# The last three attention slots of a two-part kernel reordered, and its routing cut by batch

## Chip, cores and metric

The kernel runs on one core of one Trainium2 chip. The metric is the device time of one execution in microseconds (us), the median of several runs. A core has a matrix engine (PE, with its weight loads shown as PEld), a vector engine (DVE), a scalar engine (ACT), GpSimd (POOL), SyncE (SP, which here only issues transfers) and 16 DMA engines that move data. Each engine works through its own list of instructions in order and waits on semaphores for the others. Matmul results land in PSUM, everything else lives in SBUF. "p_h<-xTt,w_all" in a profile row means that an instruction writes tile p_h and reads tiles xTt and w_all.

## What is computed

A chunked attention over 4 batches, 8 heads and 768 tokens is followed by a mixture of 8 experts with a noisy top-2 router over all 3072 tokens.

```python
for c in range(nc):                      # 24 chunks of 32 tokens; keys from 16 left to 8 right
    k_full = concat([mem_k, k[:, :, l_start:r_end]], axis=2)      # 8 memory keys + window
    scores = scale * matmul(q_c, k_full.T)
    a = softmax(scores)
    out[:, :, c_start:c_end] = matmul(a, v_full)
x = out.transpose(0, 2, 1, 3).reshape(N, D)                       # N = 3072, D = 512
noisy = x @ w_gate + log1p(exp(x @ w_noise)) * noise
top2 = the two largest of 8 per token; top2_w = softmax over the two
for e in range(E):                       # 8 experts
    h = maximum(x[mask] @ w1[e], 0.0)    # w1[e]: 512 x 1024
    out[mask] += top2_w[mask, k, None] * (h @ w2[e])              # w2[e]: 1024 x 512
```

## The kernel before, in words

Attention goes in 12 slots of 256 tokens, three to a batch: slots 0 to 2 are batch 0, and slots 9 to 11 batch 3. The rows of 128 tokens are called groups, two to a slot, 24 in all. For each slot `scores` runs 40 small matmuls into a PSUM tile ps_s, and DVE takes the row maximum (mx, L423) and subtracts it (sc, L425). `exps` is one ACT instruction (pb, L430). `turn_p` transposes the result on PE (L436), and ACT copies it to pT (L439). `values` sums the weights on PE (small, L447), multiplies with the values (ps_o, L453), and DVE normalises into xrow (L457, L460). `turn_x` transposes that on PE (L470), with a copy by ACT (xT, L472), and `gate` multiplies with the gate and noise weights (L480), whereupon DVE copies the logits to lg_all (L482). Before a batch can start, `turn` transposes its keys and queries ("turns", L393): 8 units, four of K and four of Q, each copied out by ACT or DVE (L549). There is one kT for all batches, so a batch's K copies wait until the scores of the batch before are done.

The engines PE, ACT, DVE and SP keep the order in which the program writes their instructions (a manual schedule), and POOL is pinned likewise. The loop over i = 0 to 11 at L562 is a pipeline: pass i makes the scores of slot i + 1, the turn_p of slot i, the turn_x of slot i - 1, the values of slot i, the exps of slot i + 1 and the gate of slot i - 1. `PLAN` puts the turns of the next batch into the passes; batch 3's K turns stand at the end of pass 7. ps_s and ps_o have one PSUM tile each, and all other PSUM tiles of the attention come from a ring of three (`bank`).

Routing is made in four `Route`s over groups: r0 (0 to 5), ra (6 to 13), rb (14 to 19) and rc (20 to 23). `choose` is 14 small DVE instructions that find the two experts and write a one-hot of the pair (ohp). `ranks` is a chain of small matmuls, `place` turns them into a rank per token, `total` carries the counts on, and `slots` writes a one-hot of the rank (oh_l). `weights` and `values` of a Route run on POOL or DVE. `lists` multiplies oh_l with the values into p_list on PE, and DVE adds that to `listed`. From `listed`, `decode` makes main_src, the token numbers to gather. `keep_x` writes xrow to DRAM (xd) as the source of the gathers.

POOL issues most transfers on one software queue: the loads of q, k and v, and then the weights of expert 0 before pass 6, of expert 1 before pass 7 and of expert 2 at the top of pass 8 (`load_expert`: w1 at L78, w2 at L79). Expert 2 lies in SBUF over the buffers of batch 3's K and Q, so its load waits for their turns on PE. Behind these loads POOL issues the first gathers (L671). The second part then runs step by step over pairs of experts: transposes p_xt (L691), matmuls p_h (L714) and p_y (L726).

Of the kernel before, what the change touches and what calls it, by code (L numbers as in the profile page):

```python
# [11 lines left out]
F32 = mybir.dt.float32  # L12
# [10 lines left out]
def kernel(  # L23
# [14 lines left out]
    nc = tc.nc  # L38
# [100 lines left out]
    ring = [0]  # L139
# [93 lines left out]
    class Route:  # L233
# [7 lines left out]
        def tile(self, name, width, dtype=F32):  # L241
            full = route.tile([128, self.home * width], dtype, name=f"{name}{self.home}")
            return full[:, 0:self.n * width]
# [158 lines left out]
    def scores(t):  # L402
        b, tp = divmod(t, TP)
        ps_s = psS.tile([128, 2, HP, 2, KW], F32, name="ps_s")
# [28 lines left out]
    def turn_p(pb):  # L433
# [4 lines left out]
        pT = work.tile([128, 2 * HP, 128], BF16, name="pT")  # L438
# [3 lines left out]
    def values(t, pT, between=None):  # L442
# [6 lines left out]
        ps_o = psO.tile([128, 2, HP, 2, D], F32, name="ps_o")  # L449
# [9 lines left out]
        for j in range(2):  # L459
            nc.vector.tensor_tensor(out=xr[:, j, 0:Dm].rearrange("p (h d) -> p h d", h=H),  # L460
                                    in0=ps_o[:, j].rearrange("p c a d -> p (c a) d"), in1=bc(rs[:, j], D), op=Alu.mult)
            if j == 0 and between is not None:
                between()
# [52 lines left out]
    with tc.manual_schedule(engines={ET.PE, ET.Activation, ET.DVE, ET.SP}):  # L516
# [34 lines left out]
        def fill(i, at):  # L551
            b, tp = divmod(i, TP)
            if b + 1 < B:
                turns(b + 1, PLAN[min(b, 1)].get((tp, at), ()))
# [4 lines left out]
                {(1, 1): QS[0:2], (1, 2): QS[2:4] + KS})  # L559

        r0, ra, rb, rc = Route(0, 6, 8), Route(6, 8, 8), Route(14, 6, 8), Route(20, 4, 4)
        for i in range(NT):  # L562
            b, tp = divmod(i, TP)
            last = i == NT - 1
            more = b + 1 < B

            if tp == 0 and more:
# [9 lines left out]
            if i == 2 * TP + 2:  # L577
                load_expert(2)
                ra.weights(nc.gpsimd)
                ra.order()  # L580
                ra.values(nc.gpsimd, 0, NV)
# [4 lines left out]
            if not last:  # L586
                sc = scores(i + 1)

            pTs[i] = turn_p(pbs.pop(i))
            if last:  # L590
                keep_x(b, 0, SO - 2, nc.scalar)
            elif i and tp == 0:
# [4 lines left out]
            xrs[i] = values(i, pTs.pop(i), (lambda: gate(i - 1, xTs_.pop(i - 1))) if last else None)  # L597
            if last:
                break
            pbs[i + 1] = exps(sc)  # L600
            if i in (TP + 2, 2 * TP + 2):
# [384 lines left out]
```

## Time and profile before

| what | us |
|---|---|
| median of the three runs (lowest, highest) | 358.08 (357.22, 363.62) |
| the profiled execution, its own time | 358.42 |
| its span, from the first to the last instruction | 356.7 |
| PE busy, share of the span | 285.9, 80% |
| DVE busy | 170.3, 48% |
| ACT busy | 136.9, 38% |
| POOL busy | 134.3, 38% |
| q0, the software queue that POOL issues: megabytes, share of the 16 DMA engines' time | 46.82 MB, 73.2% |
| PE p_h (L714) on the chain that ended last | 18% |
| PE p_y (L726) on that chain | 13% |

The profile is of one execution, and the durations in the text are its. The span is 1.7 us shorter than the execution's own time. A window's "DMA share" is the work of the 16 DMA engines over their time; packets can overlap, so that it can go over 1. PEclk is the share of the matrix engine's full clock that was granted.

### The profile page before, as it was taken

The numbers are of one execution on the slowest core, as the hardware profiler recorded it, in microseconds if no ns is written. First come the engines' busy times: TensorE is split into PE (matmuls) and PEld (weight loads), VectorE is DVE, ScalarE is ACT, GpSimd is POOL, SyncE is SP. The second block draws the span as 40 slices with busy tenths as digits, with TensorE's granted clock in tenths as the row PEclk, the third lists the DMA queues.
The fourth block names the chain that finished last, engine by engine and source line by source line (L and its number), as shares of the span: only waits on it lengthen the run. The fifth ranks groups of instructions, "written<-read, shape, count | busy, mean of one in ns | idle before, by whom it ended". The sixth has DMA issues, their size and how long they took to land.

```text
span 356.7 us, 7042 instructions
## 1 busy us (share of the span) xinstructions
PE 285.9 (80%) x2934; PEld 186.3 (52%) x2955; DVE 170.3 (48%) x349; ACT 136.9 (38%) x189; POOL 134.3 (38%) x181
## 2 busy tenths in 40 slices
PE   0356577777847732999999999999999999999991
PEld 0245455666736621865544465664455775565540
DVE  7656456699689885531133302954310334223221
ACT  8813645564645610144322343213243222243310
POOL 6460573354453036706530744332580122201122
PEclk9995655565687865699999999999999999999998
DMA  8999999999999999499999999961289971100012
GB/s 122 235 171 169 245 174 208 251 198 211 247 156 208 253 249 180 106 194 143 178 196 235 209 173 252 159 119 51 87 166 189 208 184 54 53 2 2 25 47 81
DMA packets 49866, 56.97 MB, mean 160 GB/s; under 512 B 16931, under 2 KB 39523, under 8 KB 49828
## 3 DMA queue, kind: packets, MB, share of 16 engines
q0 software_dynamic: 34240, 46.82, 73.2%
q1 hardware_dynamic: 13920, 6.62, 10.9%
q10 hardware_dynamic: 1668, 3.02, 2.4%
q8 instruction: 25, 0.41, 0.5%
q14 instruction: 13, 0.11, 0.1%
HBM read 70.39 MB, written 13.96 MB: 236 GB/s over the span
## 4 chain that ended last, share of the span: by engine, by line
PE 33%; issue 20%; POOL 5%; DVE 4%; DMA 3%; POOLq 1%; ACT 0%; DVEq 0%
PE p_h L714 18%; PE p_y L726 13%; POOL out_dram L677 4%; DMA out_dram<-y,main_dst 1%; DMA xTt<-xt 1%; DMA xt<-xd,main_src 1%; POOL xt L671 1%; DVE w_all L460 1%; PE p_xt L691 0%; POOL w_all L844 0%; POOLq L981 0%; DVE mx L423 0%; DVE sc L425 0%; ACT xT L472 0%; PE ps_o L453 0%
## 5 line engine op out<-in xcount | busy, mean ns | idle before, releaser
L714 PE MATMUL p_h<-xTt,w_all 128*128 128x256 bf16 (+3 forms) x669 | 102.7, 313 | 0.7 <-DVE xTt L692 0.5
L726 PE MATMUL p_y<-w_all,h 128*128 128x512 bf16 x446 | 102.3, 379 | 0.9
L714 PEld LDWEIGHTS <-w_all 128*128 128x128 bf16 x736 | 70.0, 101 | 36.3 <-issue 0.7
L702 ACT ACTIVATE h<-p_h 128x512 bf16<-128x512 f32 (+1 forms) x81 | 44.7, 551 | 95.9 <-PE p_h L714 88.3
L726 PEld LDWEIGHTS <-h 128*128 128x128 bf16 x464 | 45.3, 98 | 51.6
L700 DVE TENSOR_SCALAR h<-p_h 128x512 bf16<-128x512 f32 (+1 forms) x49 | 31.0, 633 | 82.8 <-PE p_h L714 73.7
L677 POOL DMA_INDIRECT out_dram<-y,main_dst x28 | 30.9, 1103 | 87.9 <-DVE y L732 75.4
L732 DVE SCALAR_TENSOR_TENSOR y<-p_y,main_w,y 128x512 f32<-128x512 f32 x28 | 21.0, 750 | 39.2 <-PE p_y L726 32.5
L393 PE MATMUL p_t<-identb,w_all 128*64 128x128 bf16 x384 | 20.6, 288 | 23.0 <-DMA w_all<-in_k_dram 13.4
L671 POOL DMA_INDIRECT xt<-xd,main_src x28 | 27.9, 997 | 24.2 <-DMA xTt<-xt 13.0
L730 ACT ACTIVATE y<-p_y,main_w 128x512 f32<-128x512 f32 x28 | 19.2, 687 | 37.0 <-PE p_y L726 36.0
L393 PEld LDWEIGHTS <-w_all 128*64 128x64 bf16 x384 | 18.1, 155 | 25.2 <-DMA w_all<-in_k_dram 13.9
L439 ACT COPY pT<-p_p 128x1024 bf16<-128x1024 bf16 x12 | 12.1, 1012 | 27.5 <-PE p_p L436 27.5
L383 POOL DMA_DIRECT2D w_all<-vd x16 | 11.8, 747 | 23.8 <-DMA vd<-vp 19.3
L460 DVE TENSOR_TENSOR w_all<-ps_o,rs 128x512 bf16<-128x512 f32 x24 | 15.6, 686 | 8.2 <-PE ps_o L453 7.8
L415 PE MATMUL ps_s<-kT,qT 128*32 128x112 bf16 x384 | 11.6, 276 | 7.2 <-DVE kT L549 5.4
L368 POOL COPY vp<-w_all 128x1536 bf16<-128x1536 bf16 x8 | 11.5, 1469 | 13.2 <-DMA w_all<-in_v_dram 13.2
L430 ACT ACTIVATE pb<-sc 128x1024 bf16<-128x1024 f32 x12 | 12.8, 1063 | 8.9 <-DVE sc L425 8.7
L549 DVE COPY kT<-p_t 64x768 bf16<-64x768 bf16 x12 | 11.5, 955 | 7.9 <-PE p_t L393 7.8
L425 DVE TENSOR_TENSOR sc<-ps_s,mx 128x1024 f32<-128x1024 f32 x12 | 14.7, 1225 | 0.8
L423 DVE TENSOR_REDUCE mx<-ps_s 128x16 f32<-128x1024 f32 x12 | 14.7, 1224 | 0.8 <-PE ps_s L415 0.5
L453 PE MATMUL ps_o<-w_all,pT 128*32 128x128 bf16 x384 | 10.9, 280 | 3.3 <-issue 2.0
(172 smaller groups left out, 284.0 us busy)
## 6 DMA issues: line engine op xcount, KB each, us to landing
w_all<-in_moe_w_dram POOLq DMA_DIRECT2D x16, 1024.0 KB, 20.7
w_all<-in_moe_w_dram POOLq DMA_DIRECT2D x8, 512.0 KB, 13.8
w_all<-in_v_dram POOLq DMA_DIRECT2D x4, 768.0 KB, 12.1
w_all<-in_k_dram POOLq DMA_DIRECT2D x4, 768.0 KB, 20.9
w_all<-in_q_dram POOLq DMA_DIRECT2D x4, 768.0 KB, 18.1
vd<-vp SPq DMA_DIRECT2D x4, 768.0 KB, 9.0
w_all<-vd POOLq DMA_DIRECT2D x8, 384.0 KB, 13.0
w_all<-vd POOLq DMA_DIRECT2D x8, 288.0 KB, 13.3
```

The lines of the kernel that those rows point to most:

```text
L393: nc.tensor.transpose(out=p_t[own(par), s, :], in_=src[:, 2 * pair + par, s * D:(s + 1) * D], identity=identb, tile_position=(0, par * 64))
L423: nc.vector.tensor_reduce(out=mx, in_=s3, axis=AX, op=Alu.max)
L425: nc.vector.tensor_tensor(out=sc, in0=s3, in1=bc(mx, KW), op=Alu.subtract)
L460: nc.vector.tensor_tensor(out=xr[:, j, 0:Dm].rearrange("p (h d) -> p h d", h=H), in0=ps_o[:, j].rearrange("p c a d -> p (c a) d"), in1=bc( ...
L671: i = nc.gpsimd.indirect_dma_start(out=xts[key].bitcast(I32), out_offset=None, in_=xd, in_offset=bass.IndirectOffsetOnAxis(ap=ix, axis=0))
L677: i = nc.gpsimd.indirect_dma_start(out=out, out_offset=bass.IndirectOffsetOnAxis(ap=ix, axis=0), in_=y, in_offset=None, bounds_check=N - 1 ...
L700: nc.vector.tensor_scalar(out=out_, in0=in_, scalar1=0.0, scalar2=None, op0=Alu.max)
L702: nc.scalar.activation(out=out_, in_=in_, func=Act.Relu)
L714: nc.tensor.matmul(out=o, lhsT=w(kp * F + f * 128, 128), rhs=x[:, kp], start=(kp == 0), stop=(kp == KP - 1))
L726: nc.tensor.matmul(out=p, lhsT=h[:, (f * n + j) * 128:(f * n + j + 1) * 128], rhs=w(KP * F + f * Dm, Dm), start=(f == 0), stop=(f == FB - 1))
L730: nc.scalar.activation(out=y, in_=p, func=Act.Copy, scale=weight)
L732: nc.vector.scalar_tensor_tensor(out=y, in0=p, scalar=weight, in1=y, op0=Alu.mult, op1=Alu.add)
```

## The change

Passes 0 to 7 stay as they are but for three things. `PLAN` no longer turns batch 3's K in pass 7. The second Route's noise stands ahead of the scores in pass 7, and its choice and its POOL work follow in the same pass. ps_s and ps_o share a ring of two PSUM tiles (`wide`), and pT has three buffers (pool `deep`).

From pass 8 on the loop is replaced by an order written out. Slot 8's values come first, and batch 3's K turns directly behind them (three units copied by ACT, one by DVE). Then come the load of expert 2, and the ranks of ra with the slots. Then follow the scores of slots 9 and 10, slot 11's behind slot 9's turn_p, the values of slots 9, 10 and 11, ra's lists, and the gates of slots 9, 10 and 11. The Routes are one batch each, so the third Route's logits are complete with slot 8's gate; 3 of the steps of its choice are put behind slot 10's values, and the other 11 and one more (`order`) behind slot 10's gate. Both xd writes of batch 3 and that of batch 2 are issued by SP.

```diff
-    psS = actx.enter_context(tc.psum_pool(name="psS", bufs=1))
-    psO = actx.enter_context(tc.psum_pool(name="psO", bufs=1))
+    deep = actx.enter_context(tc.tile_pool(name="deep", bufs=TP))
+    psB = actx.enter_context(tc.psum_pool(name="psB", bufs=1))
+    def wide(shape, name):
+        ring[1] += 1
+        return psB.tile(shape, F32, name=name, tag=f"ps_w{ring[1] % 2}")
-        pT = work.tile([128, 2 * HP, 128], BF16, name="pT")
+        pT = deep.tile([128, 2 * HP, 128], BF16, name="pT")
-                {(1, 1): QS[0:2], (1, 2): QS[2:4] + KS})
+                {(1, 1): QS[0:2], (1, 2): QS[2:4] + KS},
+                {(1, 1): QS[0:2], (1, 2): QS[2:4]})
-        r0, ra, rb, rc = Route(0, 6, 8), Route(6, 8, 8), Route(14, 6, 8), Route(20, 4, 4)
-        for i in range(NT):
+        r0, ra, rb, rc = (Route(b * SO, SO, b % 3 // 2) for b in range(B))
+        L0 = NT - TP
+        for i in range(L0 - 1):
...
+        i = L0 - 1
+        pT = turn_p(pbs.pop(i))
+        xTs_[i - 1] = turn_x(xrs.pop(i - 1))
+        xrs[i] = values(i, pT)
+        turns(B - 1, ((0, 1), (1, 0), (2, 1), (3, 1)))
+        load_expert(2)
+        ra.ranks()
+        gate(i - 1, xTs_.pop(i - 1))
+        p_x = turn_x(xrs.pop(i))
+        advance(ra.settle())
+        sc = [scores(L0), scores(L0 + 1)]
+        gate(i, p_x)
+        keep_x(B - 2, 0, SO, nc.sync)
+        pTs[L0] = turn_p(exps(sc[0]))
+        sc.append(scores(L0 + 2))
+        pTs[L0 + 1] = turn_p(exps(sc[1]))
+        xrs[L0] = values(L0, pTs.pop(L0))
+        pTs[L0 + 2] = turn_p(exps(sc[2]))
+        rb.noise()
+        xrs[L0 + 1] = values(L0 + 1, pTs.pop(L0 + 1))
+        chosen = rb.choose()
+        advance(chosen, 3)
+        keep_x(B - 1, 0, SO - 2, nc.sync)
+        xT = turn_x(xrs.pop(L0))
+        xrs[L0 + 2] = values(L0 + 2, pTs.pop(L0 + 2))
+        keep_x(B - 1, SO - 2, SO, nc.sync)
+        ra.lists(0, NV)
+        gate(L0, xT)
+        finish(L0 + 1)
+        xT = turn_x(xrs.pop(L0 + 2))
         advance(chosen)
         rb.weights(nc.gpsimd)
-        rb.values(nc.gpsimd, 0, 2)
-        gate(i, xT)
+        rb.order()
+        rb.values(nc.gpsimd, 0, NV)
+        gate(L0 + 2, xT)
         rc.noise()
         rb.ranks()
         advance(rb.total())
-        chosen = rc.choose()
-        advance(chosen, 4)
+        advance(rc.choose())
+        rc.values(nc.gpsimd, 0, 2)
+        rc.weights(nc.gpsimd)
+        rc.ranks()
         advance(rb.place())
-        advance(chosen)
-        rc.weights(nc.gpsimd, 0, 2)
-        rc.values(nc.gpsimd, 0, 2)
-        rc.weights(nc.gpsimd, 2, 3)
-        rc.ranks()
+        advance(rc.place())
         rb.slots(nc.vector)
         rb.lists(0, 2, more=True)
-        advance(rc.place())
         rc.slots(nc.vector, 2)
         rc.lists(0, 2, head=rb)
         src, dst = next(dec), next(dec)
-        rb.order()
         rc.order()
-        rb.values(nc.vector, 2, NV)
         rc.values(nc.vector, 2, NV)
```

`finish(t)` is `turn_x` and `gate` of slot t in a row.

More of the change, by code (lines that the diff above doesn't have):

```diff
@@ L403, in scores @@
         b, tp = divmod(t, TP)
-        ps_s = psS.tile([128, 2, HP, 2, KW], F32, name="ps_s")
+        ps_s = wide([128, 2, HP, 2, KW], "ps_s")
         for j in range(2):
@@ L448, in values @@
                              start=True, stop=True)
-        ps_o = psO.tile([128, 2, HP, 2, D], F32, name="ps_o")
+        ps_o = wide([128, 2, HP, 2, D], "ps_o")
         for j in range(2):
@@ L585 @@
                 r0.values(nc.gpsimd, 0, NV)
-            if not last:
-                sc = scores(i + 1)
+            if i == 2 * TP + 1:
+                ra.noise()
+            sc = scores(i + 1)
             pTs[i] = turn_p(pbs.pop(i))
-            if last:
-                keep_x(b, 0, SO - 2, nc.scalar)
-            elif i and tp == 0:
+            if i and tp == 0:
                 keep_x(b - 1, 0, SO, nc.scalar)
```

53 lines of the change are left out of this document (20 added, 33 removed).

## Prediction

> **What bounds the kernel now.** I read the page first, then PE's waits from 143 us on, then the windows around that point.
>
> ```profile
> PE   0356577777847732999999999999999999999991
> DMA  8999999999999999499999999961289971100012
> ```
>
> ```profile
> PE p_xt L691 <- DMA xt<-xd,main_src: 3.7, 1, 3.7
> PE p_h L714 <- DVE xTt L692: 0.5, 1, 0.5
> ```
>
> ```profile
> core 0: us, PE busy (x) PEld busy (x) DVE busy (x) ACT busy (x) POOL busy (x), PEclk, DMA share, GB/s
> 112.00:118.00 6.00, 3.59 (x120) 3.18 (x112) 5.84 (x11) 2.98 (x3) 0.00 (x0) 1.00 1.19 254
> ...
> 136.00:139.00 3.00, 0.82 (x10) 0.82 (x10) 2.48 (x10) 0.00 (x0) 1.53 (x1) 0.50 1.07 181
> 139.00:143.00 4.00, 0.30 (x4) 0.06 (x1) 0.74 (x5) 0.00 (x0) 2.98 (x4) 0.50 0.73 168
> 143.00:146.00 3.00, 2.45 (x22) 2.32 (x23) 1.87 (x8) 0.25 (x1) 2.19 (x3) 0.50 0.31 90
> 146.00:150.00 4.00, 4.00 (x36) 3.63 (x34) 2.16 (x4) 0.65 (x2) 3.61 (x5) 0.57 0.52 109
> 150.00:160.00 10.00, 9.95 (x76) 6.74 (x75) 3.41 (x6) 4.39 (x8) 1.21 (x2) 1.00 1.09 181
> ```
>
> Each digit of the first fence is 8.9 us. PE is full from the 17th digit on, and from 143 us to the end its only waits are the two of the second fence, both at the start. The expert part is thus 213.7 us of PE work (356.7 - 143.0) that the change leaves alone; the end moves only by as much as its start moves. DMA is full from the second digit to the 16th, so up to 142.6 us, and empties right when PE starts. So two paths meet at 143 us: the attention with its routing, which gives the gather its indices, and the queue of transfers. Which is last? The answers for single transfers, as issue time and time to landing:
>
> ```profile
> L79 POOL DMA_DIRECT2D w_all<-in_moe_w_dram x1: 895/895/895, 105.4 to 105.4; - x1
> ...
> DMA to landing us min/median/max: 37.2/37.2/37.2
> ```
>
> ```profile
> L671 POOL DMA_INDIRECT xt<-xd,main_src x1: 1614/1614/1614, 137.5 to 137.5; - x1
> ...
> DMA to landing us min/median/max: 5.5/5.5/5.5
> ```
>
> ```profile
> L671 POOL DMA_INDIRECT xt<-xd,main_src x1: 949/949/949, 141.9 to 141.9; - x1
> ...
> DMA to landing us min/median/max: 2.8/2.8/2.8
> ```
>
> Expert 2's second half, issued at 105.4, lands at 142.6 (105.4 + 37.2). The first gather, issued at 137.5 behind it on the same queue, lands at 143.0. The fourth, issued at 141.9, needs only 2.8. The first instruction is 1.61 long against 0.95, so without a queue ahead of it it would take about 2.8 + 0.66 = 3.5 us and land at 141.0. The queue therefore ends last, by 2.0 us, and the landing at 143.0 is a floor: bytes ahead of the gather that the change neither adds nor removes.
>
> **The change, part by part.** First, does the floor stay? The load of expert 2 now waits for K turns that come later. The K turns follow slot 8's values. They can end at about 104 (the fourth needs the room of the first, whose copy ends by then, below), and the load goes out at some 105 to 106. The queue ahead of it is long: what is issued at 105.4 lands 37 us later, and the digits and the windows (shares of 1.19 and 1.07) show the engines full up to 139. A few microseconds' delay leave no hole, cost 0; it would cost only if the queue ran empty first, tens of microseconds later. Moving the xd writes to SP and making batch 2's some 10 us earlier (it waits only for slot 8's normalising) shifts the same bytes about within a full queue, cost 0 at the end. No other transfer moves. Second, when does the gather's index come? These rows carry the sum, by shape, from the groups of 60 to 143 us:
>
> ```profile
> L460 DVE TENSOR_TENSOR w_all<-ps_o,rs 128x512 bf16<-128x512 f32 x18 | 11.7, 686 | 5.5 <-PE ps_o L453 5.2
> L472 ACT COPY xT<-p_x 128x1024 bf16<-128x1024 bf16 x9 | 9.1, 1017 | 2.4 <-PE p_x L470 2.4
> L425 DVE TENSOR_TENSOR sc<-ps_s,mx 128x1024 f32<-128x1024 f32 x7 | 8.6, 1225 | 0.5
> L423 DVE TENSOR_REDUCE mx<-ps_s 128x16 f32<-128x1024 f32 x7 | 8.6, 1223 | 0.2
> L430 ACT ACTIVATE pb<-sc 128x1024 bf16<-128x1024 f32 x8 | 8.5, 1066 | 3.8 <-DVE sc L425 3.6
> L439 ACT COPY pT<-p_p 128x1024 bf16<-128x1024 bf16 x8 | 8.1, 1012 | 17.9 <-PE p_p L436 17.9
> L549 ACT COPY kT<-p_t 64x768 bf16<-64x768 bf16 x8 | 6.4, 794 | 0.1
> ...
> L457 DVE RECIPROCAL rs<-small 128x16 f32<-128x16 f32 x8 | 2.0, 251 | 1.9 <-PE small L447 1.9
> ...
> L257 DVE TENSOR_TENSOR c<-c,desc 128x48 f32<-128x48 f32 x4 | 0.8, 208 | 0.1
> ```
>
> and these, of the timeline and of the chain:
>
> ```profile
> 96.40 1.09 ACT L430 ACTIVATE pb<-sc 128x1024 bf16<-128x1024 f32 x1
> ...
> 97.97 1.48 ACT L549 COPY qT<-p_t 128x768 bf16<-128x768 bf16 x2
> ...
> 105.69 0.66 PE L415 MATMUL ps_s<-kT,qT 128*32 128x112 bf16 x20 [1.67 <-DVE kT L549]
> ...
> 112.03 0.62 PE L436 MATMUL p_p<-identb,pb 128*128 128x128 bf16 x8
> ...
> 120.10 0.63 PE L453 MATMUL ps_o<-w_all,pT 128*32 128x128 bf16 x32
> ...
> 122.07 1.04 PE L436 MATMUL p_p<-identb,pb 128*128 128x128 bf16 x8 [0.58 <-ACT pb L430]
> ...
> 124.51 1.05 PE L453 MATMUL ps_o<-w_all,pT 128*32 128x128 bf16 x32
> ...
> 126.31 0.68 DVE L460 TENSOR_TENSOR w_all<-ps_o,rs 128x512 bf16<-128x512 f32 x1
> ...
> 128.55 0.36 PE L480 MATMUL small<-wgn,xT 128*128 128x16 bf16 x8 [1.10 <-ACT xT L472]
> ```
>
> ```profile
> 119.70 1.23 DVE sc L425
> ...
> 128.95 0.19 DVE lg_all L482
> ...
> 133.43 0.73 issue
> ...
> 135.57 0.29 PE p_list L352 x2
> ...
> 144.14 1.86 PE p_h L714 x16
> ```
>
> *Slot 8 and the K turns.* ACT sets this. From the end of slot 8's exps, 97.5, it makes two Q copies (1.48), pT (1.01), xT (1.02) and six K copies (6 x 0.79 = 4.76), and ends at 105.8. Slot 9's 40 matmuls then run in one piece, 1.3 us at the rate of the row with 20, to 107.1. Before, PE ended them at 106.35, held by DVE's K copies. Cost 0.8 us. DVE's one K unit, ra's smaller choice and ra's slots lie under ACT's time.
>
> *Scores in a row.* DVE sets this: three times mx and sc, with gaps 2.56 us each, and 0.7 for two memsets and slot 8's logits. Slot 11's sc ends at 107.1 + 7.7 + 0.7 = 115.5 against 120.9 (119.70 + 1.23), a gain of 5.4. There are two wide PSUM tiles, so slot 11's scores wait for slot 9's sc (about 110), which costs nothing, as DVE is in slot 10's until 112.5.
>
> *Values in a row.* From slot 11's sc: pb 1.07, turn_p 0.62 or 1.04 by the clock, pT 1.01, values 1.0 or 1.4 (eight matmuls as the gate's 0.36, and 0.63 or 1.05), and the normalising (0.25 and twice 0.69), 5.3 to 6.2 us, with handovers 6: 121.5. Three normalisings (4.8 us) follow 115.5 on DVE, which alone gives 120.3. I take 122, since the pT copies of three slots queue on ACT. Before it was 127.0 (126.31 + 0.68): a gain of 5.
>
> *Gates stacked up.* What was spread between the slots now stands behind the last values: ra's lists, slot 10's turn_x, copy and gate, then slot 11's. One such round is a turn of eight again (0.62 or 1.04), 1.02, 0.36 and handovers, 2.1 to 2.6 us, so that slot 10's logits come at some 124.7 and slot 11's by PE and ACT at 127. Between them DVE has the 11 steps of the third choice and `order` ahead of slot 11's logits, 12 x 0.24 = 2.8 us (0.208 and a gap of 0.03): 127.5. Before, 7 such steps lay under ACT's copy. Slot 11's logits end at 127.7 against 129.1 (128.95 + 0.19), at half clock at 128.9. Of 5 us, 1.4 are left, or 0.2.
>
> *The last Route.* Before, logits to last lists took 6.4 us (129.14 to 135.57). Now the last Route has 6 groups in place of 4. Its 14 steps of choice grow by a tenth at most (14 x 0.02 = 0.3). The gap of 0.73, in which DVE waited for the ranks, stands ahead of its place and slots, which took 1.4 (134.16 to 135.57); half more is 0.7, and I put 0.6. While PE makes those ranks, DVE had rb's slots to do and still waited 0.73; now it has rb's place, which is shorter, and PE has two matmuls more: I put 0.5 of added waiting. Cost 1.4 us.
>
> Sum: 0 at full clock, and 1.2 later at half. The first gather goes out at 137.5 to 138.7 and would land alone at 141.0 to 142.2; the floor at 143.0 covers that. The third gather must land by 146.0, where PE takes slots 1 and 2 of the expert part; 3.2 us behind the first and 3.0 long, it lands by 144.9. Net effect 0: **358.4 us**, the profiled execution's own time; the median of the runs shown is 0.3 lower.
>
> **The rivals.** *The routing overruns the floor (slower).* Place: the last gates and the two routings behind them. Each microsecond by which the first gather goes out after 139.5 (143.0 - 3.5) is lost whole. For it: margin is only 0.8 us at half clock, and DVE, ACT and PE hand over some 25 times, where 0.1 us more each is 2.5. Against: the chains above were taken with gaps. Time: 1 to 4 us late gives 359.4 to 362.4, I take 360.5. Over 2% it would need a gather at 146.7, 8 us late.
>
> *The gather is not held by expert 2.* If its 5.5 us had another cause, the first gather goes with the indices; at the best sum (1 us of handovers saved) that is 355.4 to 357.4. Against it stands the fourth gather with 2.8 us, just when the load had landed.
>
> [...]
>
> **How the numbers follow.** Floor holds 0.63, own range 357.4 to 359.4; overrun 0.20; gather free 0.07; clock 0.10. The likeliest gives 358.4. The range of 8 in 10 takes the clock case and most of the overrun: 356.6 to 361.6. A difference of 2% (7.2 us) is about what a measurement of this kernel can tell from no change. Faster by more needs the floor gone and the sum wrong by 4 us (0.03); slower by more needs the overrun at twice its upper end, one in five of its cases and a little for stalls not seen (0.05); within 2% is 0.92.
>
> **What would show it.** After the change: expert 2's second half landing at 142 to 143.5; the first gather within 0.5 us behind it; sc of slot 11 ending near 115.5 and slot 11's logits near 128; PE full from then on. A gather that goes out after 139.5 makes the overrun right; an expert 2 that lands well before 142 makes the floor wrong.

## The result and the profile after

| | kernel before | changed kernel |
|---|---|---|
| median of 22 runs each, side by side (us) | 359.94 | 362.12 |
| lowest and highest | 355.90, 363.97 | 358.99, 366.43 |
| profiled execution, own time | 358.42 | 360.29 |
| its span | 356.7 | 358.7 |

The ratio of the changed kernel to the kernel before is 1.0067, 95% interval 1.0038 to 1.0097: slower by 0.7%, less than 2%. Ratios leave disturbed runs out, so that one can differ from the quotient of two medians. The kernel before itself had medians of 358.1 to 362.5 us in different groups of runs, so that only ratios taken side by side compare.

First PE's waits of the changed kernel from 139 us on (us in total, times, longest), as in the prediction:

```profile
PE p_xt L709 <- DMA xt<-xd,main_src: 2.1, 1, 2.1
PE p_list L356 <- DVE vals L346: 1.8, 1, 1.8
PE p_h L732 <- DVE xTt L710: 0.5, 1, 0.5
```

PE still waits last for the first gathered rows (the second wait lies beside the gather). But no longer for the queue. Expert 2's second half and the first gather, issue time and time to landing:

```profile
L79 POOL DMA_DIRECT2D w_all<-in_moe_w_dram x1: 912/912/912, 106.4 to 106.4; - x1
...
DMA to landing us min/median/max: 36.4/36.4/36.4
```

```profile
L689 POOL DMA_INDIRECT xt<-xd,main_src x1: 1694/1694/1694, 141.2 to 141.2; - x1
...
DMA to landing us min/median/max: 3.6/3.6/3.6
```

The load lands at 142.8 (106.4 + 36.4), where it landed before. The gather goes out at 141.19, 3.7 us later than before, and needs 3.6 us in place of 5.5: when the instruction that issues it ends (1.69 us long, so at 142.88), the load has landed. PE starts the expert part at 144.84 in place of 143.04. From there to the end it takes 213.8 us, against 213.7 before, so the 1.8 us at the start are nearly the whole loss of this execution (1.87 us by its own time).

Where is the gather late? The timeline (start, us, engine, line, [idle before <- releaser]):

```profile
102.31 4.84 ACT L551 COPY kT<-p_t 64x768 bf16<-64x768 bf16 x6 [0.55 <-PE p_t L397]
...
107.08 0.65 PE L419 MATMUL ps_s<-kT,qT 128*32 128x112 bf16 x18
...
109.94 0.56 PE L419 MATMUL ps_s<-kT,qT 128*32 128x112 bf16 x14 [2.21 <-issue]
...
110.80 1.23 DVE L427 TENSOR_REDUCE mx<-ps_s 128x16 f32<-128x1024 f32 x1
...
118.11 1.23 DVE L429 TENSOR_TENSOR sc<-ps_s,mx 128x1024 f32<-128x1024 f32 x1
...
121.77 1.05 PE L457 MATMUL ps_o<-w_all,pT 128*32 128x128 bf16 x32
...
125.01 1.29 DVE L464 TENSOR_TENSOR w_all<-ps_o,rs 128x512 bf16<-128x512 f32 x2
...
130.06 0.18 DVE L484 COPY lg_all<-small 128x32 f32<-128x32 f32 x1
...
130.17 0.43 DVE L328 TENSOR_REDUCE red<-ohp 128x28 f32<-128x168 bf16 x1
...
130.56 1.88 POOL L346 TENSOR_TENSOR vals<-ohp,facts 128x1008 bf16<-128x1008 bf16 x1
130.63 1.85 DVE L332 TENSOR_TENSOR cum<-cum,red 128x28 bf16<-128x28 bf16 x1
132.40 0.20 DVE L269 TENSOR_TENSOR ns<-ns,nz 128x48 f32<-128x48 f32 x1
```

Two rows are strange. PE stops in the middle of slot 9's scores for 2.21 us, and waits there for nothing that the profile names ("issue"). And cum, an addition of 28 elements that took 0.24 us before, takes 1.85. It ends 0.04 us behind POOL's multiplication (130.63 + 1.85, 130.56 + 1.88).

A third thing is seen in the windows, whose seventh figure is the granted clock (the prediction shows 112 to 118 us of the kernel before). First the kernel before:

```profile
118.00:124.00 6.00, 4.25 (x91) 3.59 (x80) 4.91 (x12) 4.33 (x6) 0.00 (x0) 0.84 1.13 229
```

The changed kernel:

```profile
112.00:118.00 6.00, 2.58 (x53) 2.33 (x54) 5.02 (x7) 3.02 (x3) 0.00 (x0) 0.50 1.20 209
118.00:124.00 6.00, 5.11 (x118) 4.60 (x119) 4.08 (x8) 3.55 (x6) 0.00 (x0) 0.53 1.16 211
```

The clock is half where the kernel before had 1.00 and 0.84, and 32 matmuls of the values take 1.05 us where the row at 120.10 in the prediction has 0.63. Cut at events that both kernels have, the way to the expert part is:

| from, to (us) | before | changed |
|---|---|---|
| end of slot 8's exps, first mx of slot 9 | 9.16 | 12.27 |
| to the end of slot 9's sc | 2.49 | 2.48 |
| to the end of slot 11's sc | 11.78 | 6.06 |
| to the end of slot 11's normalising | 6.07 | 6.96 |
| to slot 11's logits | 2.15 | 3.94 |
| to the first gather's issue | 8.33 | 10.95 |
| sum | 39.98 | 42.66 |
| to PE's first row of the expert part | 5.57 | 3.64 |

Scores in a row gain 5.7 us, and nearly every other line gives some back: 3.1 ahead of them, 0.9, 1.8 and 2.6 behind them. The gather is 2.7 us later by the sum; the other 1.0 of its 3.7 is the execution's own, whose slot 8 was that much later (exps end at 98.53, against 97.49). In the other 16 traces they end at 97.4 to 101.0, so the trace of before was an early one.

### The profile page after: what moved, and what is told of

Its sections match the earlier page's. It is cut to its first block, busy times and chain, and to the rows that moved or that the text cites. A ratio compares the mean times of both kernels' runs of the same rounds, so it can differ in the third digit from the quotient of the medians.

```text
span 358.7 us, 7043 instructions
## 1 busy us (share of the span) xinstructions
PE 283.9 (79%) x2936; PEld 185.1 (52%) x2957; DVE 168.3 (47%) x346; ACT 138.8 (39%) x191; POOL 135.3 (38%) x181
## 4 chain that ended last, share of the span: by engine, by line
PE 37%; issue 20%; DVE 6%; POOL 4%; DMA 3%; ACT 2%; POOLq 1%; DVEq 0%
PE p_h L732 18%; PE p_y L744 13%; POOL out_dram L695 4%; DMA out_dram<-y,main_dst 1%; PE p_p L440 1%; DMA xt<-xd,main_src 1%; DMA xTt<-xt 1%; ACT pb L434 1%; PE p_x L472 1%; DVE w_all L464 1%; PE ps_o L457 1%; PE p_xt L709 1%; PE ps_s L419 1%; ACT pT L443 1%; DVE cum L332 1%
## 5 line engine op out<-in xcount | busy, mean ns | idle before, releaser
L440 PE MATMUL p_p<-identb,pb 128*128 128x128 bf16 x96 | 11.2, 288 | 6.2 <-ACT pb L434 6.2
```

## The experiments

My theory after this comparison: the overrun of the prediction's first rival came true, from a gap on PE, an addition held by POOL, a low clock and a longer last Route. The column before the last tests the floor, the last the whole. Each row is one trace (us), and they come from several chips; the ratio is to the kernel before in runs beside it. The five kernels with additional matmuls stand in the text alone.

| kernel | PE's gap at instruction 2753 | exps 8 to mx 9 | sc 11 to normalised | logits 11 to gather | exps 8 to gather | gather to PE's start | ratio (95%) |
|---|---|---|---|---|---|---|---|
| changed, first trace | 2.21 | 12.27 | 6.96 | 10.95 | 42.66 | 3.64 | 1.0067 (1.0038 to 1.0097) |
| changed, again | 4.15 | 14.10 | 6.96 | 10.96 | 45.29 | 3.59 | 1.0111 (1.0056 to 1.0167) |
| POOL's work split | 3.56 | 13.91 | 6.97 | 9.73 | 43.01 | 3.60 | 1.0061 (1.0023 to 1.0099) |
| scores first | 1.76 | 9.63 | 6.97 | 10.96 | 41.96 | 3.56 | 1.0057 (1.0016 to 1.0097) |
| both | 1.65 | 9.74 | 6.97 | 9.73 | 41.43 | 3.61 | 1.0026 (0.9988 to 1.0064) |
| choice early | 4.38 | 14.62 | 6.96 | 10.38 | 44.17 | 3.63 | 1.0079 (1.0039 to 1.0119) |
| transposes for the clock | 4.06 | 14.54 | 6.02 | 10.96 | 43.28 | 3.90 | 1.0032 (0.9996 to 1.0068) |
| both, and these transposes | 1.44 | 9.62 | 6.70 | 9.72 | 40.07 | 5.08 | 0.9987 (0.9958 to 1.0016) |
| before, w2 of expert 2 late | none | 9.02 | 5.96 | 8.31 | 40.65 | 3.52 | 0.9969 (0.9934 to 1.0004) |
| the same, Routes by batch | none | 8.73 | 5.65 | 9.14 | 39.55 | 3.52 | 0.9987 (0.9953 to 1.0021) |
| tuned | 2.20 | 9.40 | 6.96 | 9.48 | 40.19 | 3.55 | 0.9949 (0.9913 to 0.9986) |
| tuned, w2 early | 2.69 | 9.61 | 6.97 | 9.51 | 40.93 | 5.35 | 0.9988 (0.9956 to 1.0019) |

### cum, behind POOL

```diff
-        rb.order()
-        rb.values(nc.gpsimd, 0, NV)
+        rb.values(nc.gpsimd, 0, 2)
...
+        rb.order()
         rc.order()
+        rb.values(nc.vector, 2, NV)
```

> The changed kernel, but POOL makes only two of the six value columns of the third Route ahead of the last logits (336 elements a partition in place of 1008); DVE makes the other four behind the first list, as in the kernel before. In the changed kernel's trace DVE's 128x28 addition (cum) took 1.85 us, 130.63 to 132.48, and ended with POOL's multiplication of 1008 elements (130.56 to 132.44); elsewhere it takes 0.19. Theory POOL-holds-DVE: cum ends within 0.3 us of its sum again, the first gather goes out 1.1 to 1.6 us earlier, at 139.6 to 140.1, and the time falls by as much: 0.996 to 0.997 of the changed kernel, some 1.0035 of the kernel before. Rival (cum was late for another reason, such as a wait that the profile does not show): cum stays near 1.8 us and nothing moves. Rival (the lateness of the gather is not what sets the start of the expert part): cum is short, the gather goes out earlier, and the time stays at 1.0067 of the kernel before.

In its trace:

```profile
131.66 0.44 DVE L328 TENSOR_REDUCE red<-ohp 128x28 f32<-128x168 bf16 x1
...
131.95 0.75 POOL L346 TENSOR_TENSOR vals<-ohp,facts 128x336 bf16<-128x336 bf16 x1
...
132.14 0.60 DVE L332 TENSOR_TENSOR cum<-cum,red 128x28 bf16<-128x28 bf16 x1
```

With a third of POOL's work cum ends at 132.74, again 0.04 us behind POOL (132.70), and from the logits to the gather it takes 1.22 us less. POOL holding DVE is shown: cum took 1.85 us beside 1.88 on POOL, and 0.60 beside 0.75. The same rows in the kernel before:

```profile
128.96 0.75 POOL L342 TENSOR_TENSOR vals<-ohp,facts 128x336 bf16<-128x336 bf16 x1
129.06 0.43 DVE L324 TENSOR_REDUCE red<-ohp 128x28 f32<-128x168 bf16 x1
...
129.52 0.24 DVE L328 TENSOR_TENSOR cum<-cum,red 128x28 bf16<-128x28 bf16 x1
```

There the reduction, which reads one tile, ran under POOL's work from start to end in 0.43 us, as long as in the changed kernel, where it had ended before POOL's work was well begun. The addition reads two, and even its 0.24 us ended 0.05 us behind POOL. In all three traces cum ended 0.04 to 0.05 us behind POOL; whether the number of tiles that it reads has a part in that, no run shows. The time did not fall clear of noise, though (1.0061 against 1.0067): this execution's gap on PE was 3.56 us, 1.35 more than in the first trace, and the 1.2 us drowned in that.

### PE's gap in slot 9's scores

```diff
         load_expert(2)
+        sc = [scores(L0)]
         ra.ranks()
...
-        advance(ra.settle())
-        sc = [scores(L0), scores(L0 + 1)]
+        settle = ra.settle()
+        advance(settle, 2)
+        sc.append(scores(L0 + 1))
...
         sc.append(scores(L0 + 2))
+        advance(settle)
```

> The changed kernel, but slot 9's scores stand directly behind the K turns, ahead of the second Route's ranks, slot 7's gate and slot 8's turn_x (46 PE instructions), and the second Route's total and slots stand behind slot 11's scores on DVE. In the changed kernel's trace PE stops for 2.21 us after the 18th of slot 9's 32 narrow matmuls, and a packet of 16 KB of the queue of instructions starts in that gap (107.49, 1.18 us long). From the start of one such packet to the next PE runs some 256 instructions, and in three places of the two traces PE stops with 448 or 449 recorded instructions run since the start of the packet's block. Theory (PE runs out of instructions): PE stops at the same count, so behind slot 9's scores, among the ranks and the gate; the scores run in one piece of 1.2 to 1.4 us and end at 108 to 108.6 in place of 110.5; sc of slot 11 ends at 116.5 to 118 in place of 119.3; the first gather goes out at 139.2 to 140.2 in place of 141.2, and the time is 0.994 to 0.997 of the changed kernel. Rival (the gap belongs to slot 9's scores, as by a K copy that PE waits for unseen): the gap stays inside the scores, and nothing moves by more than 0.5 us. Rival (the later stalls swallow it: DVE's choice and cum set the gather): scores in one piece, sc of slot 11 earlier, but the gather within 0.5 us of 141.2.

PE's timeline in this trace:

```profile
107.05 0.66 PE L419 MATMUL ps_s<-kT,qT 128*32 128x112 bf16 x20 [1.35 <-ACT kT L551]
107.64 0.32 PE L292 MATMUL p_rank<-ohp,tri 128*128 128x168 bf16 x1
107.75 0.35 PE L293 MATMUL p_rank<-cum,ones 128*128 128x168 bf16 x1
107.89 0.56 PE L296 MATMUL p_rank<-ohp,ones 128*128 128x140 bf16 x5
108.29 0.20 PE L482 MATMUL small<-wgn,xT 128*128 128x16 bf16 x2
110.25 0.33 PE L482 MATMUL small<-wgn,xT 128*128 128x16 bf16 x6 [1.76 <-issue]
```

The scores run in one piece, and the gap stands in slot 7's gate. Counting PE's rows from the start of the trace (weight loads and its semaphore rows among them), it is behind number 2753 again. In all 14 traces with the changed order PE stops at this number, for 1.4 to 4.4 us, from as early as 106.9 us to as late as 111.3; in the attention, long stops that the profile calls "issue" come behind 1217 and 1985 too, and once, in the old order, behind 2497 (at 1217 a wait for semaphores stands beside, so that it is the least clear). The four lie 768, 512 and 256 rows apart. And in the gap the queue of instructions moves one packet; the DMA view of the changed kernel from 107 to 109 us (queue, packets, MB, share of 16 engines):

```profile
q0 software_dynamic: 159, 0.32, 89.0%
q1 hardware_dynamic: 25, 0.15, 19.3%
q8 instruction: 1, 0.02, 3.7%
```

It starts at 107.49, is 1.18 us long, and PE goes on 1.27 us behind its end. It is 16 KB (the page counts 25 packets on this queue, 0.41 MB), and PE has run 2753 rows when it starts and 2303 when the one before it does; in the traces of both kernels most such packets start 180 to 280 rows apart, on average 248 in the kernel before and 249 in the changed one, the last packet of each left out. So I take the gap for PE out of instructions: a packet came late, while the DMA engines were full (the three shares add up to 112%). In the old order such a packet starts at 106.04, and at 107.68 with w2 of expert 2 late, when PE has run only 2619 and 2635, so no gap appears at this place: the new order brings PE there sooner. Why the packet waits as long as it does was not tried.

The gather goes out at 140.34, just outside what I expected, and 1.0057 is less of a gain than I expected. Of the 2.6 us won ahead of slot 9's mx (9.63 in place of 12.27), 1.9 are lost again up to the end of slot 11's sc (7.98 in place of 6.06), as the gap now stands ahead of slot 10's scores, for which DVE waits 1.16 us, and two steps of the second Route have come in between.

> Both edits at once. Theory: the two gains add on the path to the gather (1.1 to 1.6 and 1.0 to 2.0 us), which goes out at 137.6 to 139.1; from 139.5 on down expert 2's second half, which lands at 142 to 143.5 ahead of it on the same queue, sets the start of the expert part, so that the first gather lands behind it at 142.5 to 143.5 and the time is that of the kernel before (0.998 to 1.002 of it), not less by the whole sum. Rival (no floor): the gather lands 3.5 us after its issue, at 141.1 to 142.6, and the time falls below the kernel before by 0.5 to 2 us (0.995 to 0.999).

Both edits together give 9.74 us up to slot 9's mx and 9.73 from the logits, the gather goes out at 139.70 and 41.43 us behind slot 8's exps, and the ratio falls to 1.0026. That misses what I expected by 0.6 us, and just behind the prediction's 139.5 the gather is not held by expert 2 (3.61 us to PE's start). Against the old order (39.98 and 40.65) 0.8 to 1.4 us are left, so something was still missing from the account. The load's last packet (its packets are the ones of 1024 bytes on the software queue) had ended at 142.16, so that it was through when that gather's rows landed.

> The changed kernel unchanged, for its trace and its time beside the other runs of this group, since each of the earlier experiments was traced once, and on another chip than the changed kernel. Theory: from slot 11's logits to the first gather 10.9 to 11.0 us pass again (10.95 in its first trace, 8.33 in that of the kernel before), cum takes over 1.7 us, the gather goes out 40.5 to 43 us after the end of slot 8's exps and PE starts the expert part 3.5 to 3.7 us behind it; ratio 1.004 to 1.010 to the kernel before. Rival (the lateness was that one execution's): the interval to the logits or from them to the gather is shorter by a microsecond or more, and the ratio is within 0.3% of 1.

The same kernel again: 10.96 us from logits to gather, cum 1.85, but a gap of 4.15 us and 45.29 in all. The size of the gap varies from execution to execution. In this trace no other piece of the lateness is as large; in the first, with 2.21, it lies nearer to the 1.61 that cum lost (1.85 less 0.24).

> The changed kernel, with one thing moved: the 11 last steps of the third Route's choice stand on DVE ahead of slot 10's logits in place of behind them. In the changed kernel's trace they ran from 127.38 to 130.06, between slot 10's logits (127.46) and slot 11's (130.24), whose matmuls had ended at 129.2. Theory (the steps are on the path): slot 11's logits follow their matmuls, 0.6 to 1.0 us earlier against the end of slot 9's normalising, and POOL's multiplication starts earlier as well, so that cum waits only some 1 us in place of 1.65; the gather goes out 0.8 to 1.6 us earlier, ratio to the changed kernel 0.996 to 0.998. Rival (ACT and PE set slot 11's logits): the logits come within 0.3 us of the same interval, and only the wait of cum gets shorter.

```diff
-        finish(L0 + 1)
-        xT = turn_x(xrs.pop(L0 + 2))
+        xT = turn_x(xrs.pop(L0 + 1))
         advance(chosen)
+        gate(L0 + 1, xT)
+        xT = turn_x(xrs.pop(L0 + 2))
```

From slot 9's normalising to slot 11's logits 8.91 us, against 9.19 and 9.97 in the two traces of the changed kernel, and cum 1.28. So the steps cost 0.3 to 1.1 us there, but the clock has a part in that: it was 1.00 from 126.60 on here, from 123.68 and from 127.07 in the two. The ratio cannot tell it under a gap of 4.38.

### The clock

> The changed kernel with 16 additional matmuls of 256 columns, whose results nobody reads, in PE's three waits ahead of the turn_p of slots 9, 10 and 11 (2.43, 0.99 and 0.89 us in the trace of the changed kernel: 9, 4 and 3 matmuls). There the granted clock was 0.50 from 106.6 to 123.7, where the kernel before had 1.00 from 111.9 to 122.1. Theory (the low clock comes from PE's waits and costs time): the granted clock is 1.00 from some 114 to 124, turn_p and the values of slots 10 and 11 take 0.62 and 0.63 in place of 1.03 and 1.05, the normalising of slot 11 ends 0.8 to 1.5 us earlier against slot 9's scores, and the gather 0.5 to 1.2 us earlier. Rival (DVE sets the pace there): the clock rises and the gather moves by less than 0.3 us. Rival (these matmuls do not raise the clock): it stays at 0.50, and the gather is later by what they delay.

This one missed its question: the additional matmuls wrote to the tile `small` and waited for DVE's copy of logits out of it. PE stood from 111.75 to 115.65, and the ratio is 1.0147 (1.0086 to 1.0207). The clock did rise, to 1.00 from 119.40 on, and from slot 11's sc to its normalising it took 6.00 us. The next one has no such wait:

```diff
-    def turn_p(pb):
+    def turn_p(pb, more=0):
         p_p = bank([128, 2 * HP, 128], BF16, name="p_p")
+        for x in range(more):
+            nc.tensor.transpose(out=p_p[:, x % 8, :], in_=identb, identity=identb)
```

> The changed kernel with 18, 7 and 6 additional transposes of a constant, which the real ones of the same tile overwrite, ahead of the turn_p of slots 9, 10 and 11; unlike the matmuls of the experiment before on this question they wait for nothing but PE. Theory (PE's waits keep the clock low, and that costs time): the granted clock is 1.00 from 114 to 117 on until 124 or later, sc of slot 11 to the end of its normalising takes 5.9 to 6.2 us in place of 6.97, and from slot 9's first mx to the gather it takes 29.4 to 30.2 us in place of 30.4 (changed kernel, first trace) and 31.2 (second). Rival (DVE sets the pace): the clock rises and that interval stays within 0.3 us of the trace of the changed kernel. The time falls by 0 to 1 us in the first case; the length of the gap in slot 9's scores, 2.2 to 4.4 us in the traces so far, moves it by more than that either way.

```profile
112.00:118.00 6.00, 4.39 (x88) 3.81 (x89) 4.11 (x5) 1.06 (x1) 0.00 (x0) 0.60 1.11 257
118.00:124.00 6.00, 4.31 (x148) 3.65 (x149) 5.23 (x9) 4.37 (x5) 0.00 (x0) 1.00 1.21 211
```

The clock is 1.00 from 116.8 on, from slot 11's sc to its normalising it takes 6.02 us in place of 6.96, and from slot 9's first mx to the gather 28.75, against 30.40 and 31.19 without the transposes, so 1.6 us or more. With transposes in PE's waits the two windows have 0.60 and 1.00 in place of 0.50 and 0.53: that the waits keep the clock low here, and that the low clock costs those 1.6 us or more, is shown. This execution's gap was 4.06 us, and the ratio with its interval reaches from no change to the changed kernel's.

The clock also fits what is seen from slot 11's normalising to its logits, where these kernels have the same order on PE. That took 3.94 us in the first trace and with the scores first, where the clock had risen 2.6 us ahead of the normalising's end, and 4.73 in the second trace and 4.92 with both edits, where it rose 0.4 us ahead of it and 0.2 behind it.

> The changed kernel with slot 9's scores first, POOL's work split, and 17 additional transposes of a constant in PE's waits ahead of the turn_p of slots 9 to 11 (4, 7 and 6). Theory (the gather of the changed kernel is late by four things: the gap in slot 9's scores, cum behind POOL, the low clock, and the longer last Route, of which only the last is left here): from the end of slot 8's exps to the gather it takes 39.8 to 40.7 us, against 39.98 and 40.65 in the two traces with the order of the kernel before and 41.43 without the transposes; the gather then lands behind expert 2, and the ratio to the kernel before is 0.997 to 1.002. Rival (a fifth thing is missing from the account): 41.2 us or more, ratio 1.001 to 1.004.

It took 40.07 us from slot 8's exps to the gather, as the theory said and between the two traces of the old order, though cum still waits 0.4 us, the last Route is the long one, and a gap of 1.44 us stands in slot 7's gate. Of the 1.36 us to the version without the transposes, 0.27 lie in slot 11's way to its normalising and 1.05 in that to its logits. So the four causes suffice for the lateness; but the two traces of the old order differ by 0.7 us, and a cause of that size could hide. The gather goes out at 137.94, is held again (5.08 us), and the ratio is 0.9987.

### The last Route, and the floor

```diff
-        r0, ra, rb, rc = Route(0, 6, 8), Route(6, 8, 8), Route(14, 6, 8), Route(20, 4, 4)
+        r0, ra, rb, rc = Route(0, 6, 8), Route(6, 6, 8), Route(12, 6, 8), Route(18, 6, 6)
```

> The kernel before with the second half of expert 2 behind the first six gathers (so that no load holds the gather), and with one part of the change: the four Routes are one batch each, so that the last has 6 groups in place of 4. Theory (the prediction's 1.4 us for the last Route): from slot 11's logits to the gather it takes 9.4 to 9.9 us in place of 8.31, and as nothing hides that here the time is 1.003 to 1.004 of the same kernel with the old Routes (0.9969 of the kernel before), that is 1.000 to 1.001 of the kernel before. Rival (the first part of the last Route hides in waits): 8.3 to 8.9 us, ratio 0.996 to 0.998.

From logits to gather 9.14 us, between the theory's range and the rival's: Routes by batch cost 0.83 us there. The time (0.9987 against 0.9969, with intervals that overlap) cannot tell it. This kernel stands on the next one, the kernel before with a load moved:

```diff
-                load_expert(2)
+                pin(nc.gpsimd.dma_start(out=w1v[:, 2], in_=moe_w1[2].rearrange("(kp p) f -> p kp f", p=128)))
...
     gathers(0, 0, 6)
+    pin(nc.gpsimd.dma_start(out=w2v[:, 2], in_=moe_w2[2].rearrange("(fb p) d -> p fb d", p=128)))
     gathers(1, 0, 2)
```

> The kernel before, in which the second half of expert 2 (w2, 1 MB) is issued behind the first six gathers; the first half stays where it was. In the trace of before this second half landed at 142.64 and the first gather, issued at 137.5, at 142.95, after 5.5 us, where a later one needed 2.8. Theory (the landing of expert 2 is the floor): now the first gather lands 3.3 to 3.8 us after its issue, at 141.0 to 141.4, PE starts at once, and the time falls by 1.5 to 2.2 us, to 0.994 to 0.996 of the kernel before. Rival (the gather's 5.5 us had another cause, such as the rows written to DRAM, or the issue itself): it lands at 143 again, ratio 1.000. Rival (the load is missed later): the expert part waits for w2 of expert 2 or for a later load, and the time rises.

PE's waits from 139 to 150 us:

```profile
PE p_list L352 <- DVE vals L342: 2.3, 1, 2.3
PE p_xt L691 <- DMA xt<-xd,main_src: 1.7, 1, 1.7
PE p_h L714 <- DVE xTt L692: 1.3, 2, 0.8
```

PE starts 3.52 us behind the gather in place of 5.57, so the floor is what the prediction took it for. The gain is 0.3%, and its interval touches no change.

### A tuned version

It takes both mended edits and the choice placed early, loads w2 of expert 2 late, and moves three more things: ra's lists go into PE's wait for slot 11's copy, their addition behind cum; rb's slots go into DVE's wait for the last ranks; and slot 10's turn_x goes ahead of slot 9's gate.

```diff
-        ra.lists(0, NV)
...
+        ra.lists(0, NV, add=False)
         gate(L0 + 2, xT)
         rc.noise()
         rb.ranks()
         advance(rb.total())
+        ra.add(0, NV)
...
         advance(rb.place())
-        advance(rc.place())
         rb.slots(nc.vector)
+        advance(rc.place())
```

> The changed kernel with all that the findings so far suggest: slot 9's scores first and POOL's work split (both as before), the third Route's choice ahead of slot 10's logits, the second Route's lists moved into PE's wait for slot 11's copy and their addition behind cum, the third Route's slots into DVE's wait for the last ranks, and the second half of expert 2 loaded behind the first six gathers. Theory: the gather's index comes with the routing alone, and no load holds it; the gather goes out at 137 to 138.3, lands 3.5 to 3.7 us later, and the time is 0.990 to 0.996 of the kernel before. Rival (the attention's own work on DVE from slot 9's scores on leaves nothing): the gather goes out at 139 to 140, ratio 0.996 to 1.002. Rival (loads that come later are missed in the expert part): PE waits for w2 of expert 2 or a later load, ratio over 1.00.

Its gather goes out at 138.40, lands free, and the ratio is 0.9949 (0.9913 to 0.9986): half a per cent faster than the kernel before. The kernel before with nothing but that load moved has 0.9969 (0.9934 to 1.0004), though, so that the new order adds anything to the moved load is not shown. With the load back in its place:

> The tuned version with the second half of expert 2 back in its place ahead of the gathers; nothing else differs. In the tuned version's trace the first gather went out at 138.40 and PE took its rows 3.55 us later. Theory (what POOL has issued ahead lands first, at 142 to 144): the gather goes out at 138 to 139 again, and PE starts 4.5 to 5.6 us behind it, 1 to 2 us later than in the tuned version; ratio 1.003 to 1.006 to the tuned version. Rival (the landing of expert 2 holds nothing): 3.5 to 3.7 us again and the same time.

PE's waits from 139 to 150 us:

```profile
PE p_xt L716 <- DMA xt<-xd,main_src: 3.1, 1, 3.1
PE p_list L356 <- DVE vals L346: 2.3, 1, 2.3
PE p_h L739 <- DVE xTt L717: 0.5, 1, 0.5
```

PE starts 5.35 us behind the gather, and the ratio is 0.9988 (its interval overlaps that of the tuned version). That a load ahead holds the gather is shown from both sides (5.35 us here, 3.55 with the load late). Where the floor lies varies, though: this gather went out at 139.74, as late as the one at 139.70 that met no hold, but here the load's last packet ended at 144.35, against 142.16 there and 142.28 in the kernel before. So the 3.1 us by which PE starts later than in the tuned version are 1.8 of the hold and 1.3 of the later gather.

Two more experiments put work on PE ahead of the expert part, to have its clock up sooner (it was 1.00 from 6.4 us behind PE's start in the kernel before, from 4.1 in the tuned version).

> The tuned version with 15 additional matmuls of 256 columns, whose results nobody reads, in PE's last two waits before the expert part (10 ahead of the last lists, 5 ahead of the first transposes of the gathered rows). In the tuned version's trace PE starts the expert part at 141.95 and the granted clock is 0.50 until 146.06; in that of the kernel before it is so from 143.04 to 149.40. [...] Rival (the first steps of the expert part wait for gathers 1.3 us apart and for copies): the clock rises and the time falls by less than 0.5 us. Rival (these matmuls do not count for the clock): nothing changes.

> The kernel before with the second half of expert 2 behind the first six gathers, and the same 15 additional matmuls in PE's last two waits. [...] Rival: the clock rises and nothing is saved, ratio 0.996 to 0.998.

In both the additional matmuls read a tile whose memory the gathered rows take over. From main_src to the gather it took 2.3 us in place of 0.84 and 0.93, and the ratios were 0.9982 (0.9945 to 1.0018) and 0.9965 (0.9938 to 0.9991). With another operand, and then with the transposes as well:

> The tuned version with 15 additional matmuls in PE's last two waits before the expert part, now with an operand whose memory nobody else takes. In the experiment before on this question they read a tile of the attention, whose place the gathered rows take over, and the first gather went out 0.84 us behind the last such matmul. [...] Rival (the clock falls again in the waits of the first steps): no gain, 0.994 to 0.998.

> The tuned version with both kinds of additional work on PE (17 transposes of a constant in its waits of the attention's end, 15 matmuls ahead of the expert part). Theory: the clock is 1.00 in the values and gates, sc of slot 11 to the end of its normalising takes 6.0 us in place of 6.96, and the gather goes out 0.5 to 1.2 us earlier against the end of slot 8's exps than in the tuned version (40.19); ratio 0.986 to 0.993 of the kernel before. Rival (DVE is full there): the interval stays within 0.3 us and the ratio is that of the version without the transposes.

The gather went out 0.84 us behind main_src again in both. With the matmuls alone the clock was 1.00 from 145.19, 3.7 us behind PE's start, 0.4 earlier than in the tuned version (4.1); it fell to 0.50 at 148.60, as the rival has it, and the ratio was 0.9926 (0.9886 to 0.9966). With the transposes as well it was 1.00 from 2.6 us behind PE's start, and the ratio 0.9987 (0.9954 to 1.0019). The transposes raised the clock to 1.00 from 117.53 to 127.77 (0.50 in the tuned version's windows from 112 to 130), but slot 11's sc to its normalising took 6.69 us, and the way to the gather got no shorter (40.40 us from exps, 40.19 in the tuned version). DVE was busy for 5.70 of the 6 us from 118 to 124, which fits the rival (DVE is full there) but does not prove it. The intervals overlap, and whether the early clock saves anything stays open.

## Why the prediction was wrong

The step that failed is the sum for the gather: "The first gather goes out at 137.5 to 138.7". It went out at 141.19, and the prediction's own margin ended at 139.5. What failed in it are two waits that it had at nothing: 2.05 us of PE's gap in slot 9's scores (3.7 in the second trace) and 1.61 us of cum behind POOL. Piece by piece, with the prediction's values as differences of its times:

| piece of the way (us) | predicted | first trace | second |
|---|---|---|---|
| slot 8's exps to the last K copy | 8.3 | 8.62 | 8.77 |
| slot 9's scores | 1.3 | 3.35 | 5.04 |
| to slot 11's sc | 8.4 | 8.84 | 8.82 |
| to its normalising | 6.5 | 6.96 | 6.97 |
| to its logits | 5.7 to 6.9 | 3.94 | 4.73 |
| to the gather | 9.8 | 10.95 | 10.95 |

- *"Slot 9's 40 matmuls then run in one piece, 1.3 us"* is wrong by 2.1 us in one trace and 3.7 in the other. They stop in the middle (2.21 and 4.15 us), by my reading for want of instructions, a term that the sum did not have. With them moved ahead of that point they did run in one piece.
- *"Cost 1.4 us"* for the last Route was 0.4 too much for what it counted and left out the rest: the 2.62 us measured are 1.61 of cum (1.85 less 0.24) and 1.0 of the other pieces, and the Routes by batch alone made 0.83 in the kernel before. That POOL's three times larger multiplication would hold an addition on DVE was missed. The trace of before showed the same elsewhere (a comparison of 6 elements, L307, took 2.49 us from 77.77 on, and POOL's copy from 77.34 took 2.88), but the prediction drew on no such row.
- *Scores in a row* (8.4, measured 8.84) and *values in a row* (6.5, measured 6.96) were right to half a microsecond a piece, at a clock of 0.50 from 106.6 to 123.7 us. *Gates stacked up* was costed 1.8 to 3.0 us too high against the first trace and 1.0 to 2.2 against the second, which by luck hid part of the other two.
- *K turns*: the last K copy came 1.35 us after the forecast 105.8, of which 1.04 is slot 8's exps, at 98.53. In the kernel before with w2 late the exps ended at 98.50 too, so that this need not be the change's doing.
- *The floor* was right: the load landed at 142.8, and PE started 5.1 to 5.6 us behind a gather that went out well ahead of the landing, or, in the table, 3.5 to 3.9 us behind one that nothing held. So was the untouched expert part in that trace.
- *The overrun*, a rival with 0.20, is what came. Its price, "each microsecond by which the first gather goes out after 139.5", gives 358.42 + 1.69 = 360.1 us against the measured 360.29. The mechanism and its rate were right, though 1.04 of the 1.69 us are the later exps of that execution, so that the close agreement is part luck. The chance was too small: the margin of 0.8 to 2.0 us was weighed against handovers, not against waits that the sum left out.
- *The clock* (0.10, and the lower end of the range, 356.6): no run shows the term that these rest on. What the runs show from PE's start of the expert part to a clock of 1.00 is 6.4 us in the kernel before and 6.2 in the changed one (150.99 less 144.84), and 3.7 and 2.6 in the last two kernels with work put ahead of it, whose ratios (0.9926 and 0.9987) have intervals that overlap the tuned version's.

The forecast of 358.4 us was also tied to one execution. The same kernel's median beside the changed one was 359.94, so of the 3.7 us to 362.12 the execution's level is 1.5 and the change 2.2.

## What to carry to other kernels

A reordering that closes up a row of dense small matmuls can also bring closer a point at which the engine stops and waits for nothing that the profile names (here row 2753, 1.4 to 4.4 us in 14 traces); look for idle time that the profile gives no releaser for, and place what is urgent ahead of it. Before a larger piece of work goes to POOL, list the DVE instructions that fall into its time (here an addition of 28 elements took 1.85 us beside 1.88 us on POOL, and 0.60 beside 0.75). And a margin behind a floor is worth only what the sum ahead of it is worth: two waits that the sum leaves out and a low clock (0.50 from 106.6 to 123.7 us) used up this one.

## What the hardware showed that was not expected

The places of the attention at which PE stopped, as I read it for want of instructions, lie at fixed numbers of the trace's count (1985, 2497 and 2753, and likely 1217, where a wait for semaphores stands beside), 768, 512 and 256 rows apart, whatever instruction stands there. At 2753 the length varied from 1.4 to 4.4 us.

In the traces of the two kernels themselves the expert part took 213.7 and 213.8 us from PE's first row. In the 16 others, on four chips, it took 214.5 to 218.3 us. Up to 3.4 us of the difference arise ahead of the first p_y, which came 10.1 to 13.6 us behind PE's first row; in nine of the traces PE stands there for 1.2 to 2.5 us with no releaser. These stops do not lie a multiple of 256 rows from the ones of the attention. Nor does the lateness of the gather set them: the kernel before with w2 late and the matmuls had the latest gather (144.12) and 214.5 us, the tuned version with the matmuls alone the second earliest (137.81) and 217.5. So the 1.0111 of the changed kernel's second run may hold more than the late gather (its expert part took 218.2). The cause was not tried and stays open.
